# Two batches of queries transposed by DMA instead of by TensorE, in a linear-attention and highway kernel with a written-out order

## The chip, the cores and the metric

The kernel runs on one core of a Trainium2 chip. Its engines are TensorE (PE, with its weight loads shown as PEld), VectorE (DVE), ScalarE (ACT), GpSimd (POOL) and SyncE (SP), which here does nothing but issue transfers. The metric is the device time of one execution in microseconds (us), as the median of several runs.

## The reference, cut to what matters

```python
# q, k, v: (8 batches, 8 heads, 576 rows, 64 columns), float32
q_s = softmax(q, axis=-1)                      # each query row over its 64 columns
k_s = softmax(k, axis=2)                       # each key column over the 576 rows
kv  = einsum('bhsd,bhse->bhde', k_s, v)        # 64 x 64 for each batch and head
a   = einsum('bhsd,bhde->bhse', q_s, kv)
x   = a.transpose(0, 2, 1, 3).reshape(4608, 512)
H   = maximum(x @ w_h, 0)
T   = 1 / (1 + exp(-(x @ w_t + b_t)))
out = T * H + (1 - T) * x                      # (4608, 512) float32
```

## The kernel before

The 4608 output rows are done as 36 tiles of 128 rows and 512 columns. A pair of batches makes nine tiles: four of the first batch, four of the second, and one that takes what is left of both. So tiles 27 to 30 belong to batch 6, tiles 31 to 34 to batch 7, and tile 35 to both.

For each batch b, `k`, `v` and `q` load 1,152 KB each on SP's queue into float32 buffers (three for each of the three inputs). `ek` takes the exponent of the keys on ACT, `vc` casts the values to half precision, `kv` multiplies the two on PE, and `kr` and `kn` (DVE) divide by the column sums and leave the 64 x 64 blocks in `kvb`. `eq` takes the exponent of the queries on ACT and leaves it as the tile `qe`. The query rows then have to be turned, so that the 64 columns of two heads lie on the partitions: `qt` does that with eight 128 x 128 PE transposes into a PSUM bank (L318 for batches 4 to 7, L323 for the first four and for the two leftover blocks), and `qc` copies the bank to SBUF (L332, on DVE or ACT) as `eq{b}_{g}`. A batch has two such groups, g = 0 and 1, of 128 x 1024 elements, and a small third one, g = 2, for tile 35 or its like. The group g holds the two tiles 2g and 2g + 1 of the batch. Four buffers hold these groups in turn.

For each tile i, `xu` multiplies the turned queries by `kvb` (L352), `rs` and `x` divide by the row sums (DVE, L361 and L367), `xt` and `xe` turn x (PE, L375, and a copy, L382), `mh` (L410) and `mt` (L402) are the two products with the weights, four matmuls of 512 columns each, `bw` puts the bias into the PSUM bank beforehand (a copy on ACT, L390, or a matmul, L392), `th` is the gate on ACT, `dd` (DVE, L430), `uu` (DVE, L444, or with `:P` two operations on POOL, L441 and L442) and `oo` (POOL, L462) put the output together, and `st` stores it from SP's queue. Most stores take a pair of tiles, from one of seven buffers (`o32`, shared with the weights at the start). `fill_n` runs n matmuls on zeros whose result nobody reads.

What each engine does, and in which order, is written out by hand in the string ORDER, one word per step; a letter after the colon picks the engine. Each engine runs its own steps in that order, and waits at a step until its inputs are there and its buffer is free. SP's queue is one of these: a transfer that waits holds back all that come after it.

Of the kernel before, what the change touches and what calls it, by code (L numbers as in the profile page):

```python
# [9 lines left out]
FP16 = mybir.dt.float16  # L10
# [3 lines left out]


ORDER = """
b_0 q_0_0 v_0_1 setupdve k_0_0 b_32 eq_0_0 bsplit setuppool fill_5 fill_8 bp v_0_0 bc qt_0_0 ek_0_1 v_0_3 ek_0_0 k_0_2
v_0_2 vc_0_3:A bw_1 vc_0_0 ek_0_2 vc_0_2 q_0_4 vc_0_1:D ek_0_3 bw_0 w_h_0 fill_8 qc_0_0 whd_1:P kv_0_0 eq_0_1 w_h_2
w_t_2 kr_0_0 whd_0:P whd_2:P w_t_0 k_1_2 v_1_2 q_1_0 k_1_0 v_1_0 fill_5 q_1_4 kn_0_0 q_2_0 k_2_0 eq_0_2 xu_0_0 v_2_0
q_3_0 rs_0_0 whc_0:A x_0_0 k_3_0 fill_4 v_3_0 kv_0_1 fill_3 kr_0_1 kn_0_1 xu_0_1 rs_0_1 xu_1_0 rs_1_0 qt_0_1 x_1_0  # L20
whd_3:P qc_0_1 xt_1_0 xu_3_0 qt_0_2 xe_1_0:D fill_1 rs_3_0 x_3_0 x_0_1 xt_3_0 xu_2_0 wtc_2:P whc_2:A mh_1_0 wtc_0:P
vc_1_3 xe_3_0:D xt_0_0 xt_0_1 mh_3_0 qc_0_2:A xe_0_1 mt_1_0 mt_0_1 dd_1 ek_1_3 rs_2_0 xe_0_0:D mt_0_0 x_2_0 xt_2_0
vc_1_2:D mh_0_0 th_1_0 mh_0_1 uu_1_0 dd_3 ek_1_2 kv_1_1 dd_0 th_0_0 oo_1_0 kr_1_1 kn_1_1 bw_3 eq_1_0 bw_2 qt_1_0
uu_0_0:P xe_2_0 ek_1_1 qc_1_0 mt_3_0 xu_5_1 rs_5_1 mh_2_0 x_5_1 xt_5_1 ek_1_0 vc_1_1:A th_3_0 xe_5_1 dd_2 vc_1_0
xu_4_1 kv_1_0 mt_2_0 kr_1_0 rs_4_1 eq_1_1 bw_5 th_2_0 kn_1_0 xu_5_0 eq_1_2 q_4_0 x_4_1 rs_5_0 x_5_0 mt_5_1 xu_4_0
qt_1_1 qc_1_1:A oo_0_0 v_4_0 xt_5_0 xe_5_0:D mh_5_1 uu_3_0:P bw_4 mh_5_0 rs_4_0 x_4_0 xt_4_1 xe_4_1:D mt_5_0 uu_2_0:P
oo_2_0 eq_2_0:F th_5_0 xu_6_0 dd_5 xt_4_0 xe_4_0:D qt_1_2 mh_4_1 mt_4_1 mt_4_0 th_4_0 oo_3_0 mh_4_0 bw_8:A rs_6_0
uu_5_0:P bw_6:A qc_1_2 ek_2_0:F x_6_0 xt_6_0 xe_6_0:D oo_5_0 xu_8_0 qt_2_0 rs_8_0 mh_6_0 q_4_9 x_8_0 dd_4 xt_8_0
xe_8_0:D xu_7_0 rs_7_0 qc_2_0 x_7_0 mt_6_0 dd_6 mt_8_0 vc_2_2:A qt_2_1 th_6_0 xt_7_0 qc_2_1:A th_8_0 vc_2_0 kv_2_0
mh_8_0 xe_7_0:D uu_6_0 kr_2_0 kn_2_0 mh_7_0 k_4_0 eq_3_0:F xu_9_0 dd_8 uu_4_0:P k_5_0 bw_7 qt_2_2 v_5_0 rs_9_0 oo_4_0  # L30
x_9_0 mt_7_0 xt_9_0 dd_7 qc_2_2:A q_5_0 xu_10_0 xe_9_0:D bw_10:A th_7_0 rs_10_0 x_10_0 oo_6_0 qt_3_0 qc_3_0 mh_9_0
bw_9:A ek_3_0:F uu_8_0:P uu_7_0:P vc_3_0 xu_12_0 st_1_1 xt_10_0 oo_8_0 rs_12_0 x_12_0 xe_10_0:D oo_7_0 mt_9_0 dd_9
qt_3_1 vc_3_2:A xu_11_0 xt_12_0 rs_11_0 x_11_0 xe_12_0:D mt_10_0 th_9_0 th_10_0 kv_3_0 uu_9_0 oo_9_0 xt_11_0 mh_10_0
xe_11_0 kr_3_0 kn_3_0 dd_10 mh_12_0 qc_3_1 xu_14_0 rs_14_0 x_14_0 bw_12:A bw_11:A mt_12_0 mh_11_0 uu_10_0:P oo_10_0
xu_13_0 eq_4_0 eq_4_1 qt_3_2 st_1_0 xt_14_0 vc_4_0 mt_11_0 dd_12 rs_13_0 th_12_0 x_13_0 qc_3_2 uu_12_0:P bw_14:A
oo_12_0 xu_15_0 rs_15_0 x_15_0 xe_14_0 th_11_0 qt_4_0 dd_11 mt_14_0 uu_11_0 xt_13_0 xu_16_0 rs_16_0 qc_4_0:A xe_13_0
x_16_0 mh_14_0 qt_4_1 xt_15_0 th_14_0 bw_13:A xu_17_0 xe_15_0:D mt_13_0 rs_17_0 x_17_0 ek_4_0:F mh_13_0 xt_16_0 eq_4_2
vc_4_2 th_13_0 k_6_0 kv_4_0 dd_14 dd_13 xe_16_0:D kr_4_0 kn_4_0 bw_15:A uu_13_0 mh_15_0 ek_5_0:F bw_16:A oo_11_0
vc_5_2:A mt_15_0 th_15_0 q_5_9 qc_4_1 xu_18_0 rs_18_0 x_18_0 v_6_0 dd_15 uu_14_0:P mh_16_0 xt_17_0 xe_17_0:D qt_4_2
mt_16_0 th_16_0 vc_5_0 dd_16 kv_5_0 oo_14_0 oo_13_0 kr_5_0 kn_5_0 qc_4_2:A mh_17_0 xt_18_0 xe_18_0:D bw_17:A uu_16_0  # L40
q_6_0 mt_17_0 eq_5_0:F xu_20_0 rs_20_0 mh_18_0 st_5_0 qt_5_1 x_20_0 dd_17 xt_20_0 bw_18:A st_3_1 th_17_0 xu_21_0
st_3_0 xe_20_0:D mt_18_0 qc_5_1:A uu_15_0:P bw_20:A rs_21_0 oo_15_0 st_5_1 x_21_0 qt_5_0 xt_21_0 dd_18 q_7_0 v_7_0
th_18_0 bw_21:A st_7_1 oo_16_0 xu_19_0 ek_6_0 uu_17_0:P oo_17_0 xe_21_0:D ek_6_2 rs_19_0 mh_20_0 mh_21_0 vc_6_0:A
x_19_0 xt_19_0 qc_5_0 xe_19_0:D xu_22_0 st_7_0 rs_22_0 x_22_0 dd_20 k_7_0 dd_21 mt_20_0 th_20_0 mt_21_0 vc_6_2
uu_18_0:P xt_22_0 kv_6_0 xe_22_0:D eq_5_2 mh_19_0 bw_19:A mt_19_0 qt_5_2 kr_6_0 kn_6_0 th_21_0 uu_21_0 xu_23_0 qc_5_2
eq_6_0:F mh_22_0 st_16_1 uu_20_0:P qt_6_0 bw_22:A st_10_1 rs_23_0 x_23_0 xt_23_0 xu_24_0 st_10_0 dd_19 mt_22_0
xe_23_0:D oo_18_0 oo_20_0 th_19_0 rs_24_0 oo_21_0 x_24_0 uu_19_0:P bw_23:A dd_22 mt_23_0 oo_19_0 qc_6_0 xt_24_0
xe_24_0:D st_21_0 xu_25_0 mh_23_0 q_6_9 rs_25_0 th_22_0 uu_22_0:P oo_22_0 mh_24_0 x_25_0 xt_25_0 dd_23 xu_26_0 dd_24
rs_26_0 th_23_0 bw_24:A mt_24_0 x_26_0 eq_7_0:F uu_23_0:P qt_7_0 st_12_0 qc_7_0 xu_27_0 q_7_9 oo_23_0 rs_27_0 x_27_0
xe_25_0 mh_25_0 st_17_0 qt_6_1 qc_6_1 bw_25:A vc_7_2:A th_24_0 xt_26_0 xe_26_0:D vc_7_0:A mt_25_0 th_25_0 uu_24_0  # L50
xu_29_0 rs_29_0 x_29_0 bw_27:A st_12_1 mh_26_0 bw_26:A xt_27_0 xe_27_0:D qt_7_1 dd_25 xu_28_0 st_8_0 uu_25_0:P st_14_1
mt_26_0 rs_28_0 ek_7_0:F dd_26 mt_27_0 oo_24_0 x_28_0 xt_29_0 kv_7_0 xe_29_0:D xt_28_0 th_26_0 uu_26_0 oo_26_0 th_27_0
kr_7_0 kn_7_0 oo_25_0 bw_29:A mh_27_0 bw_28:A mh_29_0 dd_27 qc_7_1 xu_31_0 rs_31_0 xe_28_0 x_31_0 mt_29_0 eq_7_2
eq_6_2 qt_6_2 mh_28_0 uu_27_0:P oo_27_0 qc_6_2:A dd_29 xu_30_0 st_26_0 rs_30_0 x_30_0 th_29_0 uu_29_0:P st_14_0
bw_31:A xt_31_0 xe_31_0 qt_7_2 mt_28_0 dd_28 xu_33_0 rs_33_0 x_33_0 xt_30_0 th_28_0 xe_30_0 st_16_0 uu_28_0 st_23_0
mh_31_0 oo_28_0 dd_31 bw_30:A mt_31_0 xt_33_0 xe_33_0:D xu_32_0 rs_32_0 oo_29_0 th_31_0 x_32_0 uu_31_0:P oo_31_0
mh_30_0 mt_30_0 xu_34_0 dd_30 bw_33:A st_25_0 rs_34_0 x_34_0 th_30_0 st_19_0 uu_30_0 xt_32_0 st_31_0 qc_7_2:A mt_33_0
mh_33_0 dd_33 xe_32_0 mh_32_0 th_33_0 xu_35_0 uu_33_0 xt_34_0 oo_33_0 xe_34_0:D st_33_0 bw_32:A mt_32_0 mh_34_0
rs_35_0 st_28_0 x_35_0 bw_34:A th_32_0 oo_30_0 st_30_0 dd_32 uu_32_0 oo_32_0 xt_35_0 xe_35_0 st_32_0 mt_34_0 bw_35_0
mh_35_0 dd_34 bw_35_1 mt_35_0 th_34_0 uu_34_0 oo_34_0 th_35_0 st_34_0 mt_35_1 fill_6 dd_35 uu_35_0 th_35_1 uu_35_1  # L60
oo_35_0 st_35_0 fill_4 oo_35_1:D st_35_1:A
"""


# [1 line left out]
def kernel(  # L66
# [10 lines left out]
    nc = tc.nc  # L77
    B, H, S, D = q.shape
    DM = H * D
    P = 128  # L80
# [10 lines left out]
    eqp = pool("eqp", 4)  # L91
# [25 lines left out]
    T = {}  # L117
# [67 lines left out]

    WIDE = (4, 5, 6, 7)
    MAIN = 4 * 2 * 4 * D

    def flat_q(b):
        return landing("q", b).rearrange("p c f -> p (c f)")  # L190

    def load_q(e, b, j):
        if b in WIDE:
            head = S * D
            if j == 0:
                rows = q[b].rearrange("h (m t) d -> m h (t d)", m=NP)
                for u in range(2):
                    nc.sync.dma_start(flat_q(b)[u:P:2, 0:MAIN].rearrange("p (h f) -> p h f", h=H),
                                      rows[:, :, 5 * u * D:(5 * u + 4) * D])
            else:  # L200
                src = bass.AP(q.tensor, q.offset + b * H * head + 4 * D, [[NJ * D, P], [2 * head, 4], [1, D]])
                nc.sync.dma_start(flat_q(b)[:, MAIN:].rearrange("p (c d) -> p c d", c=4), src)
            return
# [89 lines left out]
    def eq(e, b, g):  # L293
        t = once(f"qe{b}", lambda: qep.tile([P, NJ, 4, D], FP16, tag="qe", name=f"qe_{b}"))
        if b in WIDE:
            if g == 2:
                nc.scalar.activation(t[:, 8], flat_q(b)[:, MAIN:].rearrange("p (c d) -> p c d", c=4), AF.Exp)
                return
            half = slice(0, 8) if e == "F" else slice(4 * g, 4 * g + 4)
            src = flat_q(b)[:, 0:MAIN].rearrange("p (c t d) -> p c t d", c=4, t=8)[:, :, half]  # L300
            nc.scalar.activation(t[:, half].rearrange("p t c d -> p c t d"), src, AF.Exp)
# [7 lines left out]
    def qt(e, b, g):  # L309
# [3 lines left out]
        if b in WIDE and g < 2:  # L313
            main = T[f"qe{b}"].rearrange("p j c d -> p (j c d)")[:, 0:MAIN]
            main = main.rearrange("p (hh j kk f) -> p j hh kk f", j=4, hh=2, kk=2)
# [17 lines left out]
        T[f"eq{b}_{g}"] = t  # L333


    def turned_q(b, jp, n):
        return T[f"eq{b}_{jp // 2}"][:, jp % 2, n]

    def xu(e, i, k):
# [124 lines left out]
    def st(e, i, h):  # L464
# [20 lines left out]
    does = dict(  # L485
        setuppool=setup_pool, setupdve=setup_dve, bsplit=bsplit, fill=fill,
        k=load_kv("k"), v=load_kv("v"), q=load_q, w=load_w, b=load_b, bp=bp, bc=bc,
        wtc=wt_cast, whc=wh_cast, whd=wh_less_identity, ek=ek, vc=vc, kv=kv, kr=kr, kn=kn, eq=eq, qt=qt, qc=qc,
        xu=xu, rs=rs, x=x, xt=xt, xe=xe, bw=bw, mt=mt, mh=mh, th=th, dd=dd, uu=uu, oo=oo, st=st)
    with tc.manual_schedule():  # L490
        for step in ORDER.split():
            name, _, eng = step.partition(":")
# [32 lines left out]
```

## Time and profile before

| | |
|---|---|
| median of 3 runs | 119.58 us (119.39 to 120.25) |
| the profiled execution | 119.67 us, of which the span that the profile shows is 117.6 us |
| PE busy | 110.6 us (94%) |
| DVE, ACT, POOL busy | 94.3 (80%), 92.3 (78%), 91.9 (78%) us |
| transfers on SP's queue | 39.72 MB, 94.8% of the time of the 16 DMA engines |
| TensorE's granted clock | full speed in all slices but the last |

The busy time of an engine is the union of its instructions' times. The chain of work that ended last is followed back from the last instruction, at each step to what released it. The times between issue and landing of a transfer include what lies ahead of it in the queue.

### The profile page before, as it was taken

To read this page: it belongs to the slowest core of one execution; us is meant where nothing else is said; L and a number is where in the kernel's file an instruction comes from. 1 tells how busy PE (TensorE), PEld (TensorE's weight loads), DVE (VectorE), ACT (ScalarE), POOL (GpSimd) and SP (SyncE) were. 2 spreads that over 40 slices of the span, in tenths; PEclk is the share of its full clock that TensorE was granted. 3 is DMA by queue.
4 is the path that set the end of the run, shared out by engine and by line. 5 is a ranking of instruction groups with operands and counts; after the bars stand their busy time and mean duration, and the time that the engine had idled before them with its cause. 6 is when DMAs were issued, how large, how long until landed. Compare 5 with 4: busy or idle time off the path is not lost.

```text
span 117.6 us, 3461 instructions
## 1 busy us (share of the span) xinstructions
PE 110.6 (94%) x1371; PEld 63.6 (54%) x1371; DVE 94.3 (80%) x223; ACT 92.3 (78%) x130; POOL 91.9 (78%) x103
## 2 busy tenths in 40 slices
PE   5999867989999999999999999999999999999991
PEld 1354443535655666556655566666666655554450
DVE  5654685588769899997899999889989898988870
ACT  4375481798999999799999999996998987774520
POOL 5022237299999999999999999899999789996860
PEclk9999999999999999999999999999999999999999
DMA  2999999999999999999999999999999977971595
GB/s 46 393 392 380 408 396 385 378 375 384 394 389 390 389 391 362 374 355 390 389 375 383 381 363 361 395 374 380 406 403 363 279 235 180 301 283 56 210 364 173
DMA packets 22083, 40.06 MB, mean 341 GB/s; under 512 B 3250, under 2 KB 9650, under 8 KB 22068
## 3 DMA queue, kind: packets, MB, share of 16 engines
q1 hardware_dynamic: 21920, 39.72, 94.8%
q8 instruction: 10, 0.16, 0.6%
q10 hardware_dynamic: 148, 0.14, 0.4%
q14 instruction: 5, 0.04, 0.1%
HBM read 30.41 MB, written 9.44 MB: 339 GB/s over the span
## 4 chain that ended last, share of the span: by engine, by line
PE 69%; DMA 17%; DVE 8%; SPq 2%; ACT 1%; issue 1%; DVEq 0%
PE gps L410 23%; PE tps L402 22%; DMA q<-in_q_dram 11%; PE xu L352 6%; DMA v<-in_v_dram 6%; PE turned L375 5%; PE kv L268 4%; DVE x L367 4%; PE qps L323 2%; PE qps L318 2%; SPq L183 2%; PE turned L167 2%; DVE d L430 2%; ACT qe L306 1%; DVE rs L361 1%
## 5 line engine op out<-in xcount | busy, mean ns | idle before, releaser
L462 POOL TENSOR_TENSOR o<-u,x 128x512 f32<-128x512 f16 (+1 forms) x36 | 40.7, 1144 | 3.7 <-DVE u L444 2.8
L402 PE MATMUL tps<-w16t,xT 128*128 128x512 f16 (+1 forms) x148 | 36.3, 373 | 0.8 <-POOL w16t L221 0.8
L410 PE MATMUL gps<-w16h,xT 128*128 128x512 f16 x144 | 36.3, 379 | 0.0
L367 DVE TENSOR_TENSOR x<-xu,rs 128x512 f16<-128x512 f32 (+1 forms) x39 | 25.2, 649 | 2.8
L442 POOL TENSOR_TENSOR u<-g,d 128x512 f16<-128x512 f16 x21 | 24.3, 1157 | 2.5 <-DVE rs L361 0.9
L430 DVE SCALAR_TENSOR_TENSOR d<-x,gps 128x512 f16<-128x512 f16 x36 | 24.2, 678 | 1.7 <-PE gps L410 1.6
L252 ACT ACTIVATE ek<-k 128x576 f16<-128x576 f32 (+2 forms) x15 | 18.0, 1222 | 2.5 <-DMA k<-in_k_dram 2.5
L402 PEld LDWEIGHTS <-xT 128*128 128x128 f16 x148 | 13.4, 98 | 12.1 <-issue 1.1
L410 PEld LDWEIGHTS <-xT 128*128 128x128 f16 x144 | 12.8, 98 | 11.4 <-DVE xT L382 0.5
L390 ACT COPY tps<-ball 128x512 f32<-128x512 f32 x28 | 16.3, 592 | 2.4 <-DVE u L444 2.1
L258 POOL CAST v<-v 128x1152 f16<-128x1152 f32 (+1 forms) x10 | 9.5, 953 | 10.4 <-DMA v<-in_v_dram 9.9
L375 PE MATMUL turned<-idh,x 128*128 128x128 f16 x144 | 14.3, 220 | 1.0 <-DVE x L367 1.0
L352 PE MATMUL xu<-kvb,eq 128*128 128x130 f16 (+1 forms) x160 | 14.8, 224 | 0.5 <-DVE eq L332 0.2
L167 PE MATMUL turned<-blank 128*128 128x512 f16 x44 | 12.5, 431 | 1.3 <-POOL blank L149 1.3
L352 PEld LDWEIGHTS <-eq 128*128 128x128 f16 (+1 forms) x160 | 10.2, 100 | 6.5 <-DVE x L367 1.3
L424 ACT ACTIVATE th<-tps 128x512 f16<-128x512 f32 x21 | 12.3, 592 | 1.6 <-PE tps L402 1.6
L375 PEld LDWEIGHTS <-x 128*128 128x128 f16 x144 | 10.1, 98 | 6.5 <-DVE x L367 2.6
L441 POOL TENSOR_SCALAR g<-th 128x512 f16<-128x512 f16 x21 | 13.1, 622 | 0.2 <-ACT th L424 0.2
L382 DVE COPY xT<-turned 128x512 f16<-128x512 f16 (+1 forms) x27 | 10.8, 399 | 2.8 <-PE turned L375 2.5
L306 ACT ACTIVATE qe<-q 128x1024 f16<-128x1024 f32 (+2 forms) x8 | 9.2, 1160 | 4.3 <-DMA q<-in_q_dram 4.1
L426 ACT ACTIVATE tps<-tps 128x512 f32<-128x512 f32 (+1 forms) x16 | 8.9, 556 | 2.9 <-PE tps L402 2.7
L444 DVE SCALAR_TENSOR_TENSOR u<-tps,d 128x512 f16<-128x512 f32 (+1 forms) x15 | 10.0, 669 | 0.8 <-ACT tps L426 0.2
(48 smaller groups left out, 114.6 us busy)
## 6 DMA issues: line engine op xcount, KB each, us to landing
k<-in_k_dram SPq DMA_DIRECT2D x6, 1152.0 KB, 11.6
v<-in_v_dram SPq DMA_DIRECT2D x6, 1152.0 KB, 14.4
out_dram<-o SPq DMA_DIRECT2D x23, 256.0 KB, 6.3
q<-in_q_dram SPq DMA_DIRECT2D x10, 512.0 KB, 9.5
out_dram<-o SPq DMA_DIRECT2D x6, 512.0 KB, 5.5
k<-in_k_dram SPq DMA_DIRECT2D x4, 576.0 KB, 11.9
q<-in_q_dram SPq DMA_DIRECT2D x2, 1152.0 KB, 15.6
q<-in_q_dram SPq DMA_DIRECT2D x2, 640.0 KB, 10.5
```

Of the source, the lines that this page charges most:

```text
L167: nc.tensor.matmul(spare, blank[:, 0:P], blank, start=True, stop=True, skip_group_check=True)
L252: nc.scalar.activation(t[:, :, c:c + n].rearrange("p j c d -> p c j d"), T[f"k32{b}"][:, c:c + n].rearrange("p c (j d) -> p c j d", j=NJ), ...
L352: nc.tensor.matmul(dst, turned_q(b, jp, n), kvb[b % NKV][:, hh, kk], start=True, stop=True, skip_group_check=True)
L367: nc.vector.tensor_mul(t[:, k0:k1], sums(i, k)[:, :, :, 0:64], T[f"rs{i}_{k}"][:, 0:k1 - k0].unsqueeze(3).to_broadcast([P, k1 - k0, 4, D]))
L375: nc.tensor.matmul(t[:, n], T[f"x{i}"][:, n0 + n % 2:n0 + 2 * P:2], idh, is_transpose=True, start=True, stop=True, skip_group_check=True)
L390: nc.scalar.copy(t[:, cs], ball[:, cs])
L402: nc.tensor.matmul(T[gate(i, k)][:, cs], T[f"xT{i}"][:, n], w16["t"][:, n, cs], start=False, stop=(n == parts[-1] and not first), skip_gro ...
L410: nc.tensor.matmul(t, T[f"xT{i}"][:, n], w16["h"][:, n], start=(first and n == parts[0]), stop=(n == parts[-1] and not (first and len(part ...
L430: nc.vector.scalar_tensor_tensor(t, T[f"x{i}"], -0.5, T[f"gps{i}"], op0=ALU.mult, op1=ALU.max)
L441: nc.gpsimd.tensor_scalar(g, T[f"th{i}"], 1.0, 1.0, op0=ALU.add, op1=ALU.mult)
L442: nc.gpsimd.tensor_mul(t, g, T[f"d{i}"])
L462: eng.tensor_add(t[:, cs], T[f"u{i}_{h}"][:, cs], T[f"x{i}"][:, cs])
```

## The change

The queries of batches 6 and 7 are no longer turned by PE. For these two batches the steps `qt_b_0`, `qt_b_1`, `qc_b_0` and `qc_b_1` are gone, which are 32 PE transposes and four copies of 128 x 1024 elements. In their place are four steps `qd_b_g`: each is one transposing DMA on SP's queue, which reads 1024 columns of `qe` (256 KB) and writes them turned to one of the four `eq` buffers. A group now holds one half of the heads for all four tiles of its batch, so that the first tile of a batch needs both groups. The small third group stays as it was.

```diff
     MAIN = 4 * 2 * 4 * D
+    TURNED = (6, 7)
...
+    def qd(e, b, g):
+        t = T[f"eq{b}_{g}"] = eqp.tile([P, 2, 4, P], FP16, tag="eq", name=f"eq_{b}_{g}")
+        half = MAIN // 2
+        nc.sync.dma_start_transpose(t.rearrange("p a n t -> p (a n) t"),
+                                    T[f"qe{b}"].rearrange("p j c d -> p (j c d)")[:, g * half:(g + 1) * half])
+
     def turned_q(b, jp, n):
+        if b in TURNED and jp < 4:
+            return T[f"eq{b}_{n % 2}"].rearrange("p a n t -> p (a n) t")[:, 2 * jp + n // 2]
         return T[f"eq{b}_{jp // 2}"][:, jp % 2, n]
```

The whole list ORDER is new, too. Each step that stays does the same work, but places and engines differ. Counted over the list: the gates on POOL (`uu` with `:P`) go from 21 to 18, the copies of the turned x on DVE (`xe` with `:D`) from 27 to 21, the bias copies on ACT from 28 to 26 (PE does two more), the casts of the values on ACT from 8 to 4, on DVE from 2 to 3 and on POOL from 10 to 13, one of two weight casts goes from POOL to ACT, and the idle matmuls of `fill` go from 44 to 33. SP's queue from the last query load on, before and after:

```diff
- st_3_1 st_3_0 st_5_1 q_7_0 v_7_0 st_7_1 st_7_0 k_7_0 st_16_1 st_10_1 st_10_0 st_21_0 q_6_9 st_12_0 q_7_9 st_17_0
- st_12_1 st_8_0 st_14_1 st_26_0 st_14_0 st_16_0 st_23_0 st_25_0 st_19_0 st_31_0 st_33_0 st_28_0 st_30_0 st_32_0
- st_34_0 st_35_0
+ st_5_1 st_3_1 q_7_0 st_7_1 qd_6_0 qd_6_1 st_7_0 k_7_0 v_7_0 st_10_0 st_10_1 qd_7_0 qd_7_1 q_6_9 st_16_0 st_8_0
+ q_7_9 st_12_0 st_21_0 st_12_1 st_16_1 st_17_0 st_14_0 st_14_1 st_25_0 st_28_0 st_26_0 st_23_0 st_31_0 st_19_0
+ st_30_0 st_33_0 st_32_0 st_34_0 st_35_0
```

PE's steps from tile 24 to the end of batch 7's `kv`, before and after (`qt_6_0` stands just ahead of the first line of before):

```diff
- xu_24 mt_22 mt_23 xt_24 xu_25 mh_23 mh_24 xt_25 xu_26 mt_24 qt_7_0 xu_27 mh_25 qt_6_1 xt_26 mt_25 xu_29 mh_26 xt_27
- qt_7_1 xu_28 mt_26 mt_27 xt_29 kv_7
+ xu_24 mt_19 mt_22 xu_25 xt_24 mh_23 xu_26 xt_25 mt_23 mh_25 xt_26 mt_25 xu_27 mt_26 mh_24 xu_29 mt_24 xt_27 mh_26
+ xu_28 xt_29 mt_27 mh_27 kv_7
```

The two halves of the last tile, 35, swap places at the end: before, the half that POOL adds up (`oo_35_0`) has its gate first, after, the half that DVE adds up (`oo_35_1`) has.

## The prediction

> **What bounds the kernel now.** I read the page first, then the chain that ended last in order of time, then five stretches side by side, then single steps on the time line. The page:
>
> ```profile
> PE 110.6 (94%) x1371; PEld 63.6 (54%) x1371; DVE 94.3 (80%) x223; ACT 92.3 (78%) x130; POOL 91.9 (78%) x103
> ...
> DMA  2999999999999999999999999999999977971595
> ...
> q1 hardware_dynamic: 21920, 39.72, 94.8%
> ```
>
> PE is busy nearly throughout, and so are the DMA engines until some 92 us (slice 31 of 2.94 us each): two resources at their limit at once. The chain says which of them sets the end (start, length, what):
>
> ```profile
> 10.81 12.67 DMA q<-in_q_dram
> ...
> 24.61 0.62 PE qps L323 x8
> ...
> 80.07 0.45 PE qps L318 x8
> ...
> 86.44 0.45 PE qps L318 x8
> ...
> 87.98 0.45 PE qps L318 x8
> ...
> 90.84 0.45 PE qps L318 x8
> ```
>
> Up to 24.6 us the chain is a load, batch 1's queries. After that it is PE, with stretches of DVE between 41.8 and 58 us; from 58 to 112 us it lists PE pieces end to end. The four last lines are the work that goes. Now the stretches (PE, PEld, DVE, ACT, POOL busy; clock, DMA share, GB/s):
>
> ```profile
> 62.50:82.50 20.00, 20.00 (x291) 12.21 (x290) 18.31 (x41) 18.63 (x26) 19.05 (x20) 1.00 1.07 378
> 82.50:92.50 10.00, 10.00 (x95) 6.32 (x94) 9.31 (x21) 9.40 (x13) 8.72 (x10) 1.00 1.02 376
> 92.50:112.50 20.00, 20.00 (x213) 11.27 (x212) 17.68 (x36) 13.78 (x27) 17.55 (x18) 1.00 0.69 224
> ```
>
> PE has no gap in any of the three and DVE few, at full clock. The DMA engines have room only in the last one: 31% of 20 us.
>
> **The change, part by part.** PE, transposes: four groups of eight at 0.45 us in the chain rows above, 4 x 0.45 = **-1.80 us**, all on PE's gapless stretch. The 0.61 us that the time line gives for a group has the tail of the pipeline in it, which the next matmuls cover.
>
> The copies: four on DVE, from this row of the groups,
>
> ```profile
> L332 DVE COPY eq<-qps 128x1024 f16<-128x1024 f16 x12 | 8.2, 681 | 0.8 <-PE qps L323 0.4 <-PE qps L318 0.3
> ```
>
> 4 x 0.68 = 2.7 us of DVE between 82 and 96 us. I count them at 0, because PE has no gap there that they cause; were DVE the bound, they would be worth up to -2.7.
>
> The new list: adding up the rows of the steps over both lists, PE gives up 1.4 us without the idle fills (the -1.8, and two bias matmuls more at 0.22), POOL 3.4 (three gates of 0.62 + 1.16 and one cast of 1.04 fewer, three casts of values more), ACT 1.9 and DVE 1.2 (the copies and six copies of the turned x at 0.42 fewer; three `uu` at 0.69, a cast and two small copies more). Where this falls matters. Up to tile 24 (80.6 us before) PE has 0.4 us and DVE up to 0.6 us more work than before from `qt_1_0` on; PE does 1.1 us more ahead of `qt_1_0`, where it otherwise ran fills or stood. I take **0** for all up to 80 us, between -1.1 (PE keeps what it did early) and +1.0 (both additions land on the chain). The fills cost 0: they lie before the 24.6 us load, and the ten at the end stand behind PE's last real matmul.
>
> The end: the last half tile is added up by POOL (its 128x256 add has 0.67 us) in place of DVE (0.42): **+0.25**.
>
> SP's queue, where the four transposing DMAs stand. The trace has no such transfer. As bytes they are 0.26 MB each; at the 376 GB/s of the stretch that is 0.7 us, the low end. The high end is a whole issue-to-landing with nothing overlapped: 256 KB stores without a backlog landed in this (L478):
>
> ```profile
> DMA to landing us min/median/max: 2.4/3.0/11.2
> ```
>
> so 3.0 us each. Below 0.7 is excluded, as the bytes must move. I take 0.7, because the queue overlaps all its transfers and the nearest row is a 256 KB transfer in it, and keep 3.0 for the range. The Trainium skill, page "DMA: Bandwidth & Descriptors", section "Latency and other measured facts", gives DMA transposes 261 GB/s in one kernel; an estimate by it is 1.0 us each. No row here shows it.
>
> Is that hidden? The steps that matter, from the time line and the landing times:
>
> ```profile
> 77.33 1.90 ACT L301 ACTIVATE qe<-q 128x2048 f16<-128x2048 f32 x1
> ...
> 86.72 0.40 PE L352 MATMUL xu<-kvb,eq 128*128 128x130 f16 x4
> ...
> 93.46 0.78 PE L268 MATMUL kv<-v,ek 64*64 64x65 f16 x72
> ...
> 96.13 0.40 PE L352 MATMUL xu<-kvb,eq 128*128 128x130 f16 x4
> ```
>
> ```profile
> k<-in_k_dram SPq DMA_DIRECT2D x1, 1152.0 KB, 11.6
> ```
>
> These are batch 6's exponent, the first `xu` of batch 6, `kv` of batch 7, the first `xu` of batch 7, and the last key load (issued at 77.11 us, landed at 88.7, a backlog of ten us). Up to that landing the queue had moved 32.25 MB: 30.15 of loads, 2.10 of stores. I count bytes from there at 0.38 MB per us. After the change:
> - `qd_6_0` can't issue before 77.33 + 1.90 = 79.2 us, and SP stands there; behind it wait `st_7_0` (whose buffer POOL's `oo_22` needs), `k_7` and `v_7`. Ahead of it are 29.6 MB, landed at 88.7 - 2.6/0.38 = 81.8: the queue nearly drains while SP waits, a hole of up to 0.7 us. `qd_6_1` lands at 88.7 - 2.1/0.38 = 83.2. `xu_27` wants it at 86.72 less the PE work saved by then (0.5): 86.2. Slack 3.0 us.
> - `v_7` is now last, behind 0.52 MB more: 88.7 + 1.4 = 90.1, then a cast of 1.15: `kv_7` could start at 91.3. PE comes there 0.7 us earlier than before, at 92.8. Slack 1.5.
> - `qd_7_1` lands at 88.7 + 1.57/0.38 = 92.8; `xu_31` wants it at 95.4. Slack 2.6.
> - 7.1 MB are then left, mostly stores: 18.6 us, to 111.4 if the queue never starves. The last store is issued at 114.29 - 1.55 = 112.7, and 1.4 us of the 18.6 are those last stores. Slack 2.7 us: the queue comes close to being the bound, which before it was not.
>
> So the transfers cost **0** at 0.7 us each. Sum: -1.80 + 0.25 + 0 = **-1.55 us**. Against its own run that is 119.67 - 1.55 = 118.1 us (span 116.05). That run stands 0.09 above the median of the runs shown, which changes nothing: 118.1.
>
> **The rivals.**
>
> *The queue takes the bound, slower.* Place: the stores after `qd_7_1`. A transfer that costs c us in place of 0.7 delays all behind it by four times c - 0.7, beside the hole of 0.7. The slack of 2.7 is used up at c = 1.2, and the gain at c = 1.6; at 2.0 the end is 5.2 + 0.7 - 2.7 = 3.2 us later: 121.3 us. At 3.0 it is 7.2, 125.3. On the way `oo_27` and `oo_29` wait for buffers that `st_12_1` and `st_14_1` hold (their landing by bytes is 97.5 and 100.3, some one us ahead of the need). For it: the DMA engines are full up to 92 us, three chains of work have slacks of 1.5 to 3, and no row shows that a transposing transfer moves at the rate of a plain one. Against it: 31% of the last 20 us was free.
>
> *The gain goes to DVE or to the new order.* DVE stood on the chain from 41.8 to 58 us, and up to 80 us it has no less to do. With +1.0 there and half a us of waits for batch 7's values the gain is gone: 119.6 us. Against it: DVE, ACT and POOL each have less in total.
>
> *PE keeps its early lead*, 1.1 us done before batch 1's queries land: 117.0 us. Against it: DVE's part of the chain comes after it.
>
> *The blocks go one after another.* If each of the eight 128 x 128 blocks of a transfer took a small transfer's 2.2 us (the 128 KB store at the end), one is 17.6 us: `xu_31` would start at 79.7 + 35.2 + 8.3 + 35.2 = 158 us, and 21.5 us follow: some 180 us of span, 182 of time. Against it: no transfer of this trace runs so. The Trainium skill, page "VectorE: DVE Perf Modes", section "The three transpose paths", has 1309 ns for one block on this path; an estimate by that figure is 10.5 us for a transfer and some 152 us for the span. No row here shows it.
>
> That the change does nothing can be left out: the removed rows are in the chain.
>
> **How the numbers follow.** Forecast 0.38, the queue 0.31, the order 0.20, the early lead 0.08, block by block 0.03. About 1% (118.4 to 120.8) is what a measurement of this kernel can tell from no change. The forecast lies just beyond it: of its 0.38, 0.27 faster and 0.11 same. The queue: 0.29 slower, 0.02 same. The order: 0.02, 0.13, 0.05. The lead is faster, the blocks slower. So faster 0.37, same 0.26, slower 0.37. The range reaches from the early lead, 117.0, to the queue at c = 2.3 (4 x 1.6 + 0.7 - 2.7 = 4.4), 122.5; about 0.2 lies outside. The forecast's own range is 117.5 to 119.1.
>
> **What would show it.** Right: PE has some 41 matmuls fewer (32 transposes and 11 fills, two bias matmuls more), with 32 left at L318's line; no PE wait of over 0.5 us at the lines of `xu` and `kv`; `kv` of batch 7 at 92 to 93 us, the first `xu` of batch 7 at 94 to 95.5; DMA share under 0.95 in the last 10 us; each transpose at most 1.2 us of queue. Wrong: `xu` waiting on a DMA after 84 us, POOL's `oo` waiting on `out_dram`, stores landing over 5 us after issue near the end, or PE reaching tile 24 later than 81.5 us.

## The result, and the profile after

The changed kernel takes **124.94 us** (median of 4 runs, 124.43 to 126.45) against 119.48 us for the kernel before on the same chip (119.39 to 120.25): a ratio of **1.0427, 95% interval 1.0379 to 1.0475**. It is 5.5 us slower by the medians. The slowest of the four runs, 126.45 us, was in the chip's slow state: it is counted in the median and left out of the ratio. The profiled execution took 125.01 us with a span of 123.2 us, 5.6 us more than the span before, so it can be read for the loss.

The page (busy times and counts of instructions; DMA busy share in 40 slices; SP's queue with packets, MB and share; the chain that ended last, by engine):

```profile
PE 108.7 (88%) x1330; PEld 60.5 (49%) x1330; DVE 93.7 (76%) x219; ACT 90.1 (73%) x132; POOL 88.3 (72%) x99
...
DMA  3999999999999999999999999939999899899982
...
q1 hardware_dynamic: 26144, 40.77, 97.0%
...
DMA 49%; POOL 23%; SPq 13%; PE 6%; issue 3%; ACT 1%; DVE 1%; POOLq 1%
```

Every engine has less to do than before (PE 1.9 us less, POOL 3.6), and the time is longer. The DMA row points at the reason: it has one hole (slice 27, from 80.1 us) and is then nearly full to the end, where before it fell off after 92 us. The queue moved 1.05 MB more, in 4,224 more packets, about 250 bytes each. The chain was PE before; now PE has 6% of it.

The same three stretches as before, and two shorter ones (PE, PEld, DVE, ACT, POOL busy; clock, DMA share, GB/s):

```profile
62.50:82.50 20.00, 19.90 (x293) 11.73 (x291) 18.28 (x41) 18.98 (x29) 17.88 (x19) 1.00 0.97 342
82.50:92.50 10.00, 9.99 (x78) 5.44 (x77) 8.35 (x19) 8.91 (x16) 8.37 (x9) 1.00 0.99 281
92.50:112.50 20.00, 17.39 (x192) 9.26 (x190) 14.66 (x31) 14.10 (x26) 15.65 (x16) 1.00 0.98 268
80.00:85.00 5.00, 4.99 (x42) 2.58 (x41) 4.69 (x11) 4.88 (x8) 4.92 (x6) 1.00 0.62 145
110.00:120.00 10.00, 6.23 (x46) 3.40 (x42) 6.75 (x14) 3.65 (x8) 6.75 (x8) 1.00 0.99 384
```

From 82.5 to 92.5 us the DMA engines are as busy as before (0.99 against 1.02) and move 281 GB/s in place of 376: **busy, but slow**. A share near one is not a rate. From 110 to 120 us they run at full rate, 384 GB/s: the queue is behind and catches up. PE has 2.6 us without work between 92.5 and 112.5 us, where it had none.

Not all of the slowness lies in the transposes. In these two stretches, the first of the changed kernel and the second of the kernel before, the queue has mostly stores and no transpose:

```profile
100.00:109.00 9.00, 7.95 (x61) 4.46 (x62) 6.36 (x14) 5.24 (x11) 6.91 (x7) 1.00 0.89 252
```

```profile
98.00:101.00 3.00, 3.00 (x28) 1.81 (x27) 2.57 (x6) 2.63 (x5) 2.84 (x4) 1.00 0.97 183
```

The kernel before has a slow stretch too, where its queue has room to spare. No run here shows why these stretches are slow, nor how much of the loss the longer one makes.

SP's time line (start, length, what it issued) shows the issuing engine standing in the transposes:

```profile
75.15 0.61 SPq L490 DMA_DIRECT2D out_dram<-o  x1
81.40 2.72 SPq L339 DMA_TRANSPOSE eq<-qe  x2
...
85.49 0.89 SPq L182 DMA_DIRECT2D v<-in_v_dram  x1
...
87.94 8.48 SPq L339 DMA_TRANSPOSE eq<-qe  x2
96.88 0.39 SPq L202 DMA_DIRECT2D q<-in_q_dram  x1
```

Between 75.8 and 81.4 us SP issues nothing: it waits for batch 6's exponent. Then each pair of transposes occupies SP for 2.7 and 8.5 us, where each of the two loads between them takes 0.6 to 0.9. (Other transfers can hold SP as well: the two stores issued from 69.32 us took 4.09.) The last values, `v_7`, are issued at 85.49 and land 9.2 us later, at 94.7. What comes of that (the four steps shown of before):

```profile
79.47 1.90 ACT L301 ACTIVATE qe<-q 128x2048 f16<-128x2048 f32 x1
...
88.02 0.40 PE L360 MATMUL xu<-kvb,eq 128*128 128x130 f16 x4
...
96.00 0.77 PE L268 MATMUL kv<-v,ek 64*64 64x65 f16 x72 [1.49 <-POOL v L258]
...
98.67 0.40 PE L360 MATMUL xu<-kvb,eq 128*128 128x130 f16 x4
```

Batch 6's exponent is 2.1 us later than before, the first `xu` of batch 6 1.3 us, `kv` of batch 7 2.5 us (it waits for POOL's cast of `v_7`), the first `xu` of batch 7 2.5 us. The rest is lost behind them, at the stores. POOL's waits (total, times, longest) and the end of the chain:

```profile
POOL o L470 <- DMA out_dram<-o: 6.9, 6, 2.0
```

```profile
100.28 5.39 DMA out_dram<-o
...
109.81 4.82 DMA out_dram<-o
115.15 4.52 DMA out_dram<-o
```

POOL's last step of a tile waited six times for a store to free its buffer; before it never did. The last store is issued at 120.50 us (before, 114.29).

### The profile page after: what moved, and what is told of

It is laid out like the page before. It is cut to its first block, busy times and chain, and to the rows that moved or that the text cites. A ratio compares the mean times of both kernels' runs of the same rounds, so it can differ in the third digit from the quotient of the medians.

```text
span 123.2 us, 3392 instructions
## 1 busy us (share of the span) xinstructions
PE 108.7 (88%) x1330; PEld 60.5 (49%) x1330; DVE 93.7 (76%) x219; ACT 90.1 (73%) x132; POOL 88.3 (72%) x99
## 2 busy tenths in 40 slices
DMA packets 26307, 41.11 MB, mean 334 GB/s; under 512 B 7474, under 2 KB 13874, under 8 KB 26292
## 4 chain that ended last, share of the span: by engine, by line
DMA 49%; POOL 23%; SPq 13%; PE 6%; issue 3%; ACT 1%; DVE 1%; POOLq 1%
DMA v<-in_v_dram 22%; DMA out_dram<-o 20%; POOL o L470 12%; DMA w32h<-in_moe_w_h_dram 8%; SPq L182 6%; POOL v L258 5%; POOL u L450 4%; SPq L205 4%; POOL g L449 2%; PE tps L410 2%; PE gps L418 1%; PE kv L268 1%; SPq L210 1%; SPq L490 1%; ACT v L258 1%
## 5 line engine op out<-in xcount | busy, mean ns | idle before, releaser
L258 POOL CAST v<-v 128x1152 f16<-128x1152 f32 (+1 forms) x13 | 12.3, 961 | 16.5 <-DMA v<-in_v_dram 16.5
L450 POOL TENSOR_TENSOR u<-g,d 128x512 f16<-128x512 f16 x18 | 20.8, 1155 | 1.7 <-DVE rs L369 0.3
L398 ACT COPY tps<-ball 128x512 f32<-128x512 f32 x26 | 15.1, 592 | 2.6 <-DVE u L452 2.3
L434 ACT ACTIVATE tps<-tps 128x512 f32<-128x512 f32 (+1 forms) x19 | 10.6, 560 | 4.2 <-PE tps L410 4.0
L452 DVE SCALAR_TENSOR_TENSOR u<-tps,d 128x512 f16<-128x512 f32 (+1 forms) x18 | 12.0, 668 | 1.8 <-POOL o L470 1.2
L432 ACT ACTIVATE th<-tps 128x512 f16<-128x512 f32 x18 | 10.6, 597 | 2.7 <-PE tps L410 2.2
L449 POOL TENSOR_SCALAR g<-th 128x512 f16<-128x512 f16 x18 | 11.1, 618 | 2.0 <-ACT th L432 2.0
L390 ACT COPY xT<-turned 128x512 f16<-128x512 f16 (+1 forms) x18 | 10.3, 570 | 2.6 <-PE turned L383 2.6
L166 PE MATMUL turned<-blank 128*128 128x512 f16 x33 | 9.7, 447 | 1.4 <-POOL blank L148 1.3
L390 DVE COPY xT<-turned 128x512 f16<-128x512 f16 (+1 forms) x21 | 8.1, 385 | 3.6 <-PE turned L383 3.3
```

The lines of the kernel that those rows point to most:

```text
L258: copy(v16[b % NV][:, c:c + n, :, 0:D], T[f"v32{b}"][:, c:c + n].rearrange("p c (j d) -> p c j d", j=NJ))
L390: copy(t[:, 2 * k0:2 * k1], T[f"xtps{i}"][:, 2 * k0:2 * k1])
L398: nc.scalar.copy(t[:, cs], ball[:, cs])
L450: nc.gpsimd.tensor_mul(t, g, T[f"d{i}"])
```

## The experiments

### What the transfers cost: none, plain, in pieces, transposed

Three variants keep the changed kernel's list and differ only in `qd`. With the changed kernel itself they make a ladder.

No transfer:

```diff
     def qd(e, b, g):
-        t = T[f"eq{b}_{g}"] = eqp.tile(...)
-        nc.sync.dma_start_transpose(...)
+        pass
     def turned_q(b, jp, n):
         if b in TURNED and jp < 4:
-            return T[f"eq{b}_{n % 2}"]...
+            return fixed
```

> The changed kernel without the four transposing DMAs and without anything in their place: the products of batches 6 and 7 read a fixed tile of ones instead of turned queries, a part of the computation left out. The queue theory expects 117 to 119 us (PE has 1.8 us less than in the kernel before, the queue neither wait nor bytes more). The list theory expects 122 to 125 us.

Measured: 120.16 us (119.65 to 120.76), ratio 1.0046 [1.0021, 1.0071]. This is above the range of the queue theory and below that of the list theory. With all transposing gone the new list is still not faster than the kernel before.

Plain copies of the same 256 KB, at the same places, with the same wait for the exponent:

```diff
-        nc.sync.dma_start_transpose(t.rearrange("p a n t -> p (a n) t"), ...)
+        nc.sync.dma_start(t.rearrange("p a n t -> p (a n t)"), ...)
```

> The changed kernel, with each transposing DMA replaced by a plain DMA of the same 256 KB from the same place to the same place (the two batches' queries are then not turned, so that part of the computation is left out). The same waits and bytes stay. If the rate and the queue's being held by a transpose cost most of the 5.5 us, 120 to 122 us; if the bytes and the wait for the exponent cost it, 123.5 to 125 us, the same as the changed kernel; the list theory expects 124 to 125.5 us.

Measured: 120.47 us (119.39 to 121.33), ratio 1.0059 [1.0025, 1.0094]. Its DMA row of the hole:

```profile
80.00:85.00 5.00, 5.00 (x36) 2.58 (x34) 4.66 (x10) 4.87 (x8) 4.92 (x6) 1.00 0.47 166
```

The hole is there, even deeper by its share, and together with 1 MB more of transfers it costs 0.3 us, which the two intervals do not tell from nothing. So neither SP's wait nor the bytes make the loss: the queue has the room that the prediction saw, if it keeps its rate. SP does not stand in the second pair, where the transposes held it 8.48 us:

```profile
86.99 1.20 SPq L339 DMA_DIRECT2D eq<-qe  x2
```

Plain copies, each row cut into eight pieces of 256 bytes, near the size of the changed kernel's added packets (7,410 packets under 512 bytes against the changed kernel's 7,474):

```diff
-        nc.sync.dma_start_transpose(t.rearrange("p a n t -> p (a n) t"), ...)
+        nc.sync.dma_start(t[:, :, 0:P], src.rearrange("p (n t) -> p n t", n=8))
```

> The changed kernel with each transposing DMA replaced by a plain copy of the same 256 KB in 256-byte pieces (nothing is turned in batches 6 and 7, that part of the computation is left out). If the packets' size is what made the transposes slow, 122.5 to 125 us; if it is the transposing itself and its hold on SP's queue, 120 to 121.5 us, as with plain copies of whole rows (120.5).

The pieces go to padded buffers of their own. Measured: 123.63 us (122.8 to 124.14), ratio 1.0328 [1.0271, 1.0385]. The ladder, by medians: no transfer 120.16, plain **+0.3**, in pieces **+3.2**, transposed **+1.3**; the transfers cost 4.8 us in all. The last step has the widest interval: the ratios 1.0328 and 1.0427 are each known to about half a per cent. The step of the pieces is not the price of small packets alone, since SP stands in the second pair too, and in the load behind it:

```profile
87.20 4.62 SPq L340 DMA_DIRECT2D eq<-qe  x2
91.86 4.00 SPq L202 DMA_DIRECT2D q<-in_q_dram  x1
```

### The transfers by themselves

A kernel with nothing but an exponent and transfers, of which there is one execution: eight transposes back to back, eight plain copies of the same size, eight copies in pieces, then two pairs of transposes among loads of 1,152 KB, and stores of zeros.

```python
for i in range(8): turn(turned[i], i % 2)
for i in range(8): nc.sync.dma_start(plain[i], turned[7]...)
for i in range(8): nc.sync.dma_start(piece[i][:, :, 0:P], plain[7]...)
for i in range(4): load(i)
turn(late[0], 0); turn(late[1], 1)
for i in range(4, 6): load(i)
turn(late[2], 0); turn(late[3], 1)
...
```

> A kernel that computes nothing of the reference: one load, one exponent, then on SP's queue eight transposing DMAs of 128 x 1024 elements back to back, eight plain copies of the same 256 KB, eight copies in 256-byte pieces, and then 1,152 KB loads with two pairs of transposes among them. If a transpose costs the queue 1.3 us where a plain copy costs 0.7 (as the changed kernel's trace suggests: two of them in 2.7 us), the first eight take 10 to 11 us and the plain eight 5.5 to 6; if the small packets are the reason, the eight in pieces take 9 to 11 us as well, if not 6. If a transpose holds SP until its data moves, SP stands 8 us or more at the second transpose behind four loads; if not, under 2 us.

SP's time line, and the rates in a stretch of transposes and in one of plain copies (last column GB/s):

```profile
8.19 10.97 SPq L47 DMA_TRANSPOSE turned<-qe  x8
20.98 5.09 SPq L56 DMA_DIRECT2D plain<-turned  x8
28.17 8.22 SPq L58 DMA_DIRECT2D piece<-plain  x8
...
40.29 12.46 SPq L47 DMA_TRANSPOSE late<-qe  x2
...
53.96 7.49 SPq L47 DMA_TRANSPOSE late<-qe  x2
```

```profile
10.00:18.00 8.00, 0.00 (x0) 0.00 (x0) 0.00 (x0) 1.00 1.00 189
22.00:27.00 5.00, 0.00 (x0) 0.00 (x0) 0.00 (x0) 1.00 0.99 369
```

Eight transposes take 10.97 us of SP, **1.37 us each**; a plain copy 5.09 / 8 = 0.64. The engines show the same share (1.00 and 0.99) at half the rate. The pieces lie between: 215 GB/s in the page's slices, 0.26 MB / 215 GB/s = 1.2 us each. Each of the eight transposes also holds SP for 1.32 to 1.34 us, so this row does not tell whether the DMA engines or the issuing sets their rate. In one stretch behind loads, from 53 to 54 us, two transposes moved 287 GB/s.

With four loads ahead of them in the queue, two transposes hold SP for 12.46 us, 8.85 of them in the first; with two loads ahead it is 7.49. SP comes free at 52.75 us, and the rate of the loads, some 390 GB/s, ends at about 52. So for a pair the hold lasts about until the loads ahead have moved, while the first transpose alone let go earlier. SP issues nothing behind them meanwhile. From 52 to 55 us the queue then moves 197 GB/s at a share of 1.13: these are mostly the transposes' own packets. It runs low for half a us at their end (a share of 0.48 from 54.5 to 55). What in the queue makes SP stand was not tested.

### The hole closed

The last key load and a store go ahead of the first two transposes, so that the queue has work while SP waits for the exponent.

```diff
- st_5_1 st_3_1 q_7_0 st_7_1 qd_6_0 qd_6_1 st_7_0 k_7_0 v_7_0 ...
+ st_5_1 st_3_1 q_7_0 k_7_0 st_7_1 st_7_0 qd_6_0 qd_6_1 v_7_0 ...
```

> The changed kernel with its transposing DMAs, where the last key load and one store are issued ahead of the first two transposes, so that the queue has 1.4 MB to move while SP waits for the exponent. The trace of the changed kernel has a hole of 2.4 us there. If a late queue is what costs, the time falls by the hole, 1.5 to 2.5 us, to 122.5 to 123.5 us. If the hole is hidden, 124.5 to 125.5 us.

Measured: 122.63 us (121.96 to 122.95), ratio 1.0244 [1.0194, 1.0294], 2.3 us better than the changed kernel. The stretch of the hole:

```profile
80.00:85.00 5.00, 4.99 (x44) 2.66 (x43) 4.78 (x10) 4.87 (x8) 4.82 (x6) 1.00 1.18 349
```

349 GB/s in place of 145. A hole that cost next to nothing with plain copies seems worth some 2 us here. The edit changed something else besides: the second pair of transposes holds SP for 6.20 us in place of 8.48, so not all of the 2.3 us need be the hole's. Queue time has a price only where the queue sets the end. The rest of the loss stays, and POOL still waits 4.4 us for stores.

### More buffers for the output

Ten buffers for pairs of tiles in place of seven, to tell the buffers from the queue.

```diff
-    op = pool("op", 7)
+    op = pool("op", 10)
```

> The changed kernel with ten output pair buffers in place of seven, and its transposing DMAs. In its trace GpSimd waits 6.9 us in all for stores to free a buffer. If that is how the late queue reaches the end (GpSimd, then DVE and PE stop), 122 to 123.5 us. If the last bytes in the queue are the end whatever the engines do, 124.3 to 125.3 us.

Measured: 125.52 us (124.9 to 126.95), ratio 1.0521 [1.0458, 1.0583]: no gain. The wait goes,

```profile
POOL o L470 <- DMA out_dram<-o: 2.9, 2, 2.1
```

from 6.9 to 2.9 us, and the last store is issued at 120.37 us, where it was 120.50. From 110 to 120 us the queue is full, at 392 GB/s. POOL's waits were a symptom; the queue's last bytes are the end.

### Batch 7 alone, with the old list

The list of before; only batch 7's two groups are turned by DMA, behind the last query load, where before the queue had room.

```diff
- qt_7_0 ... qc_7_0 ... q_7_9 oo_23_0 ... qt_7_1 ... qc_7_1
+ q_7_9 qd_7_0 qd_7_1 oo_23_0 ...
```

> The kernel before with its own list, where batch 7's queries alone are turned by two transposing DMAs, issued behind the last small query load, 10 us ahead of their use. PE has 0.9 us less, DVE 1.36. If the queue has room for two transposes there (31% of its last 20 us was free), 118.4 to 119.2 us; if SP's being held behind them makes the stores late enough for GpSimd to wait for buffers, 119.5 to 122 us.

Measured: 119.59 us (118.94 to 120.5), ratio 0.9997 [0.997, 1.0024]. Half of the change in a better place costs nothing and brings nothing, though 0.9 us of transposes and two copies are gone. In its trace the two transposes hold SP for 5.83 us (from 89.57), and the first `xu` of batch 7 waits twice for them, 0.53 and 0.55 us. This profiled execution, 120.5 us, was the slowest of the ten, so these waits may be smaller in the others. But `kv` of batch 7, which comes ahead of them, starts at 93.25 us against 93.46 before: only 0.21 us of the 0.9 had been gained by then. The rest had to be looked for where the gain was expected.

### The gain by itself, with the old list

The list of before without the transposes and copies of both batches, and with no transfer.

```diff
- qt_6_0 qt_6_1 qt_7_0 qt_7_1 qc_6_0 qc_6_1 qc_7_0 qc_7_1   (each at its place)
+ (nothing; turned_q returns a fixed tile for these groups)
```

> The kernel before with its own list, where the four groups of transposes and four copies of batches 6 and 7 are left out, and their products read a fixed tile of ones, a part of the computation left out. It does the same work as the changed kernel without transfers (120.16 us), in the old order. If the new list is at fault for that kernel's being no faster than before, 117.3 to 118.3 us (the 1.8 us of PE are then saved whole). If the removal itself is worth nothing, 119 to 119.8 us.

Measured: 119.23 us (118.9 to 119.65), ratio 0.9972 [0.9952, 0.9991]. **Taking 1.8 us off PE and 2.7 us off DVE is worth 0.2 to 0.3 us** (the interval is 0.1 to 0.6). PE's time line, at three places where a group of transposes stood (the bracket is the idle time that the profile reports):

```profile
80.52 0.40 PE L379 MATMUL turned<-idh,x 128*128 128x128 f16 x4 [0.23 <-DVE x L371]
...
86.76 0.41 PE L356 MATMUL xu<-kvb,fixed 128*128 128x130 f16 x4
...
91.18 1.89 PE L406 MATMUL tps<-w16t,xT 128*128 128x512 f16 x8 [0.32 <-ACT tps L394]
...
93.24 0.92 PE L270 MATMUL kv<-v,ek 64*64 64x65 f16 x72
```

At 80.52 PE now waits for DVE's x of tile 23. At 86.76 the product ahead began at 85.58 and takes 0.86 us at PE's rate, so about 0.3 us are idle; the chain has DVE's x of tile 26 ending at 86.71 there. At 91.18 it waits for ACT's bias copy. Each of these waits had been covered by the transposes. The bracket counts from the modelled end of the last matmul; counted at PE's rate from the starts, as for 86.76, the three waits are about 0.4, 0.3 and 0.5 us, two thirds of the 1.8. `kv` of batch 7 starts 0.22 us earlier than before (93.46), in place of 1.8 (`kv` of batch 6 had begun 0.34 us later in this profile, 76.47 against 76.13, so PE made up 0.56 us between the two), and the last `xu` at 107.14 against 107.22.

### Is it ACT that keeps the gain?

ACT shows no gap there from 83 to 95 us, and the exponent of batch 7's keys on it ends just before `kv_7`. Three kernels took four things off ACT: the bias copies of tiles 25 to 27 (to PE) and the copy of the turned x of tile 25 (to DVE).

```diff
- bw_25:A ... bw_26:A ... bw_27:A ... xe_25_0
+ bw_25 mt_25_0 ... bw_26 mt_26_0 ... bw_27 mt_27_0 ... xe_25_0:D
```

On the kernel without the transposes:

> The kernel before without the turning of batches 6 and 7 (as in the run of 119.23 us, its products read a fixed tile), and with ACT relieved between 85 and 91 us: the bias of tiles 25, 26 and 27 is set by PE (three matmuls of 0.22 us, just ahead of each tile's products) in place of three ACT copies, and one copy of the turned x goes to DVE; ACT has 2.2 us less there, PE 0.65 more, DVE 0.42 more. If ACT, which reaches the last exponent of the keys no sooner without the transposes, is what holds the 1.8 us back, 118.0 to 118.8 us. If the limit is elsewhere (DVE, or the loads), 119.0 to 119.6 us.

On the kernel with batch 7 alone turned by DMA:

> The kernel with batch 7 alone turned by two transposing DMAs (119.59 us), with the same four moves off ACT. If ACT held the gain back and two transposes fit into the queue, 118.4 to 119.2 us; if the two transposes' time on the queue is what cancels the gain, 119.3 to 120.5 us.

On the kernel before:

> The kernel before with the same four moves off ACT and with its 32 transposes. If PE and ACT bind together between 80 and 94 us, PE's 0.65 us more count in full: 119.4 to 120.2 us. If ACT alone bound, it would fall to 118.0 to 118.8 us as well.

Measured: 121.02 us, ratio 1.0110 [1.0081, 1.0139]; 121.21 us, 1.0118 [1.0090, 1.0146]; 122.38 us, 1.0227 [1.0190, 1.0263]. All slower, beyond what either theory had expected. But the moves did something else besides: in the first, PE waits 1.43 us at 89.08 us for the copy of tile 25's x, which on DVE came behind the steps of tile 27. So the moves were done again without that copy, first on the kernel without the transposes:

```diff
- bw_25:A ... bw_26:A ... bw_27:A
+ bw_25 mt_25_0 ... bw_26 mt_26_0 ... bw_27 mt_27_0
```

> The list of before, the eight-block transposes of batches 6 and 7 and their copies left out, the first eight queries' groups of these batches read from a fixed tile of ones (so batches 6 and 7 are not computed from their queries); and the bias copies of tiles 25, 26 and 27 done as one matmul each on PE just ahead of the products, which takes 3 x 0.55 = 1.65 us off ACT between 83 and 93 us and puts 3 x 0.22 = 0.66 us on PE. If ACT took the bound when PE's transposes went (theory), the exponent of batch 7's keys ends 1.0 to 1.6 us earlier, kv of batch 7 starts at 91.9 to 92.4 us in place of 93.24, and the time is 118.0 to 118.6 us (ratio about 0.990). If the stretch is held by DVE or by the order of PE's steps (rival), kv of batch 7 stays within 0.3 us of 93.24 and the time is 119.0 to 119.9.

and then on the kernel before:

> The kernel before with only the bias copies of tiles 25, 26 and 27 done on PE: ACT 1.65 us less, PE 0.66 us more in a stretch where PE has no gap. If PE alone binds there: 0.4 to 0.7 us slower, 119.9 to 120.2. If ACT and PE bind in turn: within 0.3 us of before.

Measured: 119.47 us (119.22 to 119.85), ratio 0.9979 [0.9959, 1.0], and 120.89 us (120.81 to 121.49), ratio 1.0107 [1.0078, 1.0136]. In the first, ACT now waits for PE three times between 89 and 94 us (0.2 to 0.5 us), where it had no gap, the wait of PE at 91.18 is gone, and `kv_7` starts at 93.39. The waits for DVE at 80.52 and 86.76 are as they were. So ACT alone isn't what holds the stretch: relieved by 1.65 us, it gives way to PE at once, which got 0.66 us more. In the second, the same 0.66 us on PE costs 1.1 us by the medians (119.75 for before in that comparison), more than either expectation had; the 0.4 us over the work itself stay unexplained. **What was taken off PE brought almost nothing, and what was put on it was paid for.**

### The new list

The kernel with nothing turned takes 119.23 us with the old list and 120.16 with the new one: the list costs about 0.9 us. One try to find where: the chain with the new list goes through POOL from 39 to 63 us, so two casts of values went from POOL to ACT.

```diff
- vc_3_2 ... vc_4_2
+ vc_3_2:A ... vc_4_2:A
```

> The new list, no transfer, queries of batches 6 and 7 from a fixed tile of ones as in e4 (so these two batches are not computed from their queries); and two casts of values (the second half of batch 3's and of batch 4's, 1.11 us each on POOL at 47 and 59 us) done by ACT. If POOL is what the new list loses by (theory): the values' load of batch 6 is issued at 61.2 to 62.4 us in place of 63.51, kv of batch 6 starts at 76.1 to 76.6 in place of 77.27, and the time is 119.2 to 119.7 us against e4's 120.16. If the loss lies elsewhere, in the queue's bytes or in ACT, which gets 2.2 us more (rival): kv of batch 6 stays within 0.2 us of 77.27 and the time is 120.0 to 120.6.

Measured: 121.50 us (121.34 to 121.61), ratio 1.0160 [1.0140, 1.0179]. The load went out earlier (62.79 us), by less than expected, but `kv` of batch 6 began 0.9 us later (78.18): the chain now runs through ACT from 56.5 to 65.2 us. So relieving POOL at ACT's cost does not bring the loss back. Whether POOL is what the list loses by stays open, since this edit loaded ACT.

A last variant keeps the new list and turns on PE at the places of `qd`:

```diff
- qd_6_0 ... qd_6_1 ... qd_7_0 ... qd_7_1
+ qt_6_0 qc_6_0 ... qt_6_1 qc_6_1 ... qt_7_0 qc_7_0 ... qt_7_1 qc_7_1
```

> The new list, with the 32 TensorE transposes and the four copies (on VectorE) put back at the places of the four transposing DMAs. The queue theory (the transposing DMAs and the hole ahead of them make SP's queue the bound, and the list itself is sound) expects 118.5 to 120.5 us. The list theory (the new list is itself 4 to 5 us worse, whatever turns the queries) expects 123 to 125.5 us.

Measured: 125.31 us (125.02 to 125.48), ratio 1.0473 [1.0434, 1.0512]. This lies in the range of the list theory, but it doesn't separate the list from the transfers, and 120.16 us with the same list and nothing turned speaks against that theory. A place that suits SP's queue doesn't suit PE: there PE waits 1.01 us at `qt_6_0` for the copy `qc_5_2` on ACT, and `qc_7_1` stands ahead of `kr_7` on DVE (the first `xu` of batch 7 came at 101.86 us). It is inconclusive.

## Why the prediction was wrong, step by step

It forecast 118.1 us and got 124.94. The rival that came true is the first one, the queue as the bound, and of the "wrong" signs that it named, POOL's `oo` waiting on `out_dram` is in the trace (6.9 us). PE's wait of 1.49 us at `kv_7` is over the 0.5 us that it allowed. The sign by the DMA share failed: over the last ten us of the span it is 0.75, under the 0.95 named, because the queue has little left in the last three us; from 110 to 120 us it is 0.99. The rival was right in kind and too small: with the measured 1.37 us for c, its own formula puts the end only 4 x 0.67 + 0.7 - 2.7 = 0.7 us later, at 118.8 us.

- **PE's transposes, -1.80: failed.** Worth 0.2 to 0.3 us together with the copies. The step took "PE has no gap" and "the chain lists PE" to mean that PE time is end-to-end time. The chain names one releaser at each step; DVE's x and ACT's bias copies were due close behind, under the transposes' cover, and PE waited 0.3 to 0.5 us for them at each place once the cover was gone. The copies at 0 fit the same measurement.
- **The new list, 0 between -1.1 and +1.0: mis-sized.** About +0.9, near the upper end of its bounds. In the profiles without any turning PE begins `kv` of batch 6 at 77.27 us with the new list and at 76.47 with the old one, so most of it seems lost by then; over all profiles it is 76.5 to 77.6 with the new list (seven) and 76.0 to 76.8 with the old one (eight), so a single pair can't carry the size. The sums of busy time per engine (all lower) said nothing of it. Which engine it is stays open.
- **The last half on POOL, +0.25: right.** From the end of the last product to the last store's issue it is 115.55 - 113.85 = 1.70 us with the new list and nothing turned, and 114.29 - 112.87 = 1.42 before: +0.28.
- **The transfers at 0.7 us each: failed.** 1.37 us each, back to back and alone. The nearest row was chosen by bytes; the row needed was one by packet size. The Trainium skill, page "DMA: Bandwidth & Descriptors", section "Latency and other measured facts", has 261 GB/s in one kernel, by which the estimate was 1.0 us; the measured 189 GB/s is below it.
- **The hole, 0.7 us: mis-sized.** The exponent ended at 81.4 and not 79.2 us. At a share of 0.62 in 80 to 85 us some 1.9 us of queue are lost, and the variant that fills it, with SP held less later on, gains 2.3 us.
- **SP held by a transpose: missing.** The prediction let SP issue on while a transpose waits its turn in the queue. In fact SP stands still, 8.5 us at the second pair.
- **The slack at the queue's end, 2.7 us: used up.** It was right that there was slack: plain copies at the same places cost 0.3 us.
- **Break-even at c = 1.6: wrong, for two reasons.** It counted on a gain of 1.55 us, of which nothing was there with the new list, and it put the price of a transpose only into its own transfer. Against plain copies at 0.7 us, four transposes at 1.37 are 2.7 us more; the runs show 4.5. The rest may lie in SP's hold and in the slow stretch from 100 to 109 us; no run parts the two.

In sum, by medians: 120.16 - 119.48 = +0.7 for the new list without any turning (its 0.9 less the 0.2 that the removed work brings), and +4.8 for the transfers, is the 5.5 us measured. The rival "block by block" is excluded: eight blocks take 1.37 us back to back, 0.17 us for each (the Trainium skill, page "VectorE: DVE Perf Modes", section "The three transpose paths", has 1309 ns for one; no run here timed a single block).

No variant that does the whole work beats the kernel before; batch 7 alone is level with it (0.9997). Two that leave out the transposing come out below it, and even they gain 0.3% at most.

## What to carry to other kernels

Before counting work taken off the engine that the chain names as a gain, look at when the second and third engine deliver at each place where the work stood: in this kernel, balanced by hand, the cover beneath was a few tenths of a us deep. Price a transfer also by its packets and by what it does to the engine that issues it, not by bytes alone, and read a DMA share together with its GB/s. The hole in the queue cost next to nothing while the queue did not set the end, and up to about its length where it did.

## What the runs showed of the hardware that was not expected

- Eight transposing DMAs of 256 KB, one behind the other on one queue, moved 189 GB/s; eight plain copies of the same size 369 GB/s, at the same busy share; eight copies in 256-byte pieces about 215 GB/s.
- SP, which issued the transposing DMAs, stood in a pair of them about until the loads ahead in its queue had moved: 12.46 us for two behind four loads of 1,152 KB, 7.49 us behind two. Plain copies behind a backlog did not do this in the kernel with plain copies (1.20 us for two). Copies in pieces did in part (4.62 us for two, and 4.00 us for the load behind them).
- The DMA engines' busy share doesn't tell their rate: stretches with shares of 1.02 and 0.99 moved 376 and 281 GB/s.
